# A seam in seven steps: its second transpose two slots ahead of its halves, and one product moved from GpSimd to VectorE

## Chip, cores, metric

One Trainium2 chip, one core. The metric is the device time of one execution in microseconds (us). The engines are called PE (TensorE), PEld (its weight loads), DVE (VectorE), ACT (ScalarE) and POOL (GpSimd).

## The reference

Induced attention on four sequences, then an RMS-normalised SwiGLU feed-forward layer on all 49,664 tokens, in fp32 (condensed):

```python
# x (4, 12416, 128), inducing (32, 128); w_gate, w_val (128, 1536); w_out (1536, 128)
def mab(q, kv):
    s = scale * (q @ kv.transpose(0, 2, 1))
    s = s - s.max(-1, keepdims=True)
    a = np.exp(s)
    a /= a.sum(-1, keepdims=True) + 1e-09
    return a @ kv
h = mab(I, x)            # 32 rows per sequence
y = mab(x, h)            # back to 12416 rows; then, on (49664, 128):
rms = np.sqrt(np.mean(y * y, axis=-1, keepdims=True) + 1e-06)
xn = y / rms * rms_g
g = xn @ w_gate
return ((g * (1.0 / (1.0 + np.exp(-g)))) * (xn @ w_val)) @ w_out
```

As `y` is a combination of 32 rows of `h`, the kernel multiplies `h` with the gate and value weights once per sequence. The feed-forward loop then needs only the attention weights `a` of each token, scaled so that the row of `y` that they make has an RMS of 1. Making those scaled weights is the seam.

## The kernel before

The seam of one group of 2048 tokens, as six steps. Each step is put into the instruction stream at a position of the group before: one pass of the loop below is a slot, and the 48 slots of a group are its positions 0 to 47. The last step makes the two halves, hi and lo, of the turned weights.

```python
def seam(b, s):
    ...
    engine = nc.gpsimd if b or s else nc.vector
    ...
    def turn_a():
        eT = st["eT"] = work.tile([P, 512], F32, name="eT", tag="work")
        nc.vector.transpose(out=eT[rows, 0:w], in_=sc[b][rows, cols2[s]])

    def square():
        ...
        nc.tensor.matmul(ps[rows, 0:w], gram[b][rows, rows], st["eT"][rows, 0:w], start=True, stop=True)

    def turn_z():
        ...
        nc.vector.transpose(out=z[rows, :, :].rearrange("p t m -> p (t m)"), in_=ps[rows, 0:w])
        engine.tensor_tensor(out=z[rows, :, :], in0=z[rows, :, :], in1=weights(b, s), op=ALU.mult)

    def scale():        # sum of z, then ms ** -0.5 on POOL
        ...
        nc.gpsimd.tensor_tensor(out=rs, in0=ms, in1=mhalf[rows, 0:n], op=ALU.pow)

    def apply():        # weights *= rs, in place in sc
        ...
        engine.tensor_tensor(out=a, in0=a, in1=rs.unsqueeze(2).to_broadcast(...), op=ALU.mult)

    def split():
        aT = work.tile([P, 512], F32, name="aT", tag="work")
        nc.vector.transpose(out=aT[rows, 0:w], in_=sc[b][rows, cols2[s]])
        ...
        nc.scalar.copy(out=hi[rows, 0:w], in_=aT[rows, 0:w])          # the cast of hi, on ACT
        ...
        engine.tensor_tensor(out=lo[rows, 0:w], in0=aT[rows, 0:w], in1=hi[rows, 0:w].bitcast(F32), op=ALU.subtract)

    return [turn_a, square, turn_z, scale, apply, split]
```

The loop body, and the operands of a split projection:

```python
def three(j, t):
    ...
    nc.scalar.activation(hi, v, AF.Copy, scale=1.0 - 2.0 ** -13)                    # ACT
    nc.gpsimd.tensor_tensor(out=lo, in0=v, in1=hi.bitcast(F32), op=ALU.subtract)    # POOL
    def rest():
        hs = third.tile([P, 512], F32, name="hs")
        nc.scalar.activation(hs[:, 0:T], hi.bitcast(F32), AF.Copy, scale=1.0 + 2.0 ** -12)
        nc.gpsimd.tensor_tensor(out=d, in0=hs[:, 0:T], in1=v, op=ALU.subtract)      # POOL, the third operand
        kara.append((ready[b, u, j], lambda: project3(j, hi, lo, d)))
    soon(1, rest)

for j in range(NJ):                                   # one slot
    nc.tensor.matmul(g[:, 0:T], sg[:, ts(j, P)], a[:, 0:T], start=True, stop=True)      # gate
    nc.scalar.activation(sl[:, 0:T], g[:, 0:T], AF.Silu)
    products(j)                                       # projections that are due
    nc.tensor.matmul(v[:, 0:T], sv[:, ts(j, P)], a[:, 0:T], start=True, stop=True)      # value
    nc.vector.tensor_tensor(out=t[:, 0:T], in0=sl[:, 0:T], in1=v[:, 0:T], op=ALU.mult)  # u
    steps(j)                                          # seams, prologue of the next sequence, ...
    ...
```

Where the steps stand, and the build-time reckoning of POOL's time that decides which projections are split (`SLOT` 1.25 us, `SPLIT` 2.75 us):

```python
j = ((14, 17, 18, 21, 21, 33) if k else (32, 33, 33, 34, 34, 37))[i]
...
seam_busy[at] = seam_busy.get(at, 0) + {2: 1.4, 3: 3.0, 4: 1.2, 5: 1.4}.get(i, 0)
...
free = max(free, now) + busy.get(k, 0) + seam_busy.get((b, u, j), 0)
begin = max(free, now + 2.2 * SLOT)
if (j not in KJ or b == 0 and u < 2 or (b, u) == flat[-1] or begin > now + 3.2 * SLOT or
        any(k - 2 <= e <= k + 6 for e in marks)):
    continue                                          # stays plain
free = begin + SPLIT
ready[b, u, j] = int((free + 0.3) / SLOT) + 1
```

## Time and profile before

| | before |
|---|---|
| time, median of 4 runs | 1710.03 us (1708.84 to 1710.2) |
| span of the profiled execution | 1708.1 us, granted clock 0.995 |
| busy share | PE 98%, ACT 72%, DVE 67%, POOL 67% |
| first gate matmul | 59.8 us after the start |
| ACT's cast of hi waiting for the turn | 40.2 us in 27 waits |

Most of these rows say little about where a microsecond can be had: PE looks full. One more place matters below, the first seam inside the loop. Lines of the timeline, before (start and duration in us; the bracket is the wait ahead of the instruction and what ended it):

```profile
131.21 2.90 POOL L499 TENSOR_TENSOR rs<-ms,mhalf 128x16 f32<-128x16 f32 x1
...
134.19 1.05 POOL L503 TENSOR_TENSOR sc<-sc,rs 128x512 f32<-128x512 f32 x1
135.20 1.26 POOL L603 TENSOR_TENSOR xn<-hs,u 128x512 fp32r<-128x512 f32 x1
...
136.52 0.50 PE L560 MATMUL acc<-xn,xn 128*128 128x512 f32 x1 [2.69 <-POOL xn L603]
```

PE stands still for 2.69 us for the third operand of a split projection, which stood behind the seam's power and apply in POOL's queue. Below I call this the standstill.

### The profile page before, as it was taken

Reading aid. Unit: us, or ns where it says so; the run is one execution under the profiler, and the core shown is the slowest. Engines: PE = TensorE matmul, PEld = TensorE weight load, DVE = VectorE, ACT = ScalarE, POOL = GpSimd, SP = SyncE. Lnnn points to the kernel's source line nnn. Section 1 sums busy time; section 2 is a strip of 40 time slices with the busy share of each in tenths; the row PEclk is TensorE's granted clock in tenths of the full one; section 3 lists DMA queues with packets and bytes.
Section 4 is the critical chain, followed back from the end, with each engine's and each line's share of the span. In section 5 each row is a group of like instructions: output and inputs, shape, how many; then the busy total and the mean of one; then the engine's idle time right before and its main releaser. Section 6 shows DMA issues by size and latency. Waiting matters only on the chain.

```text
span 1708.1 us, 23142 instructions
## 1 busy us (share of the span) xinstructions
PE 1668.0 (98%) x6781; PEld 1036.0 (61%) x6781; DVE 1145.0 (67%) x1914; ACT 1224.3 (72%) x2179; POOL 1146.2 (67%) x919
## 2 busy tenths in 40 slices
PE   8799999999999999999999999999999999999998
PEld 7445565655566666665556666566556666666666
DVE  4767775676667776667666777566756666666665
ACT  4446777676787777766678777767677887788786
POOL 1217775677587777677658777577657878887774
PEclk9899999999999999999999999999999999999999
DMA  6344533533354332433335314153211111111111
GB/s 261 74 68 75 70 80 60 121 75 69 56 78 68 49 65 51 105 75 88 65 57 90 57 34 87 28 131 79 54 31 33 35 36 33 33 36 36 33 37 24
DMA packets 389358, 112.64 MB, mean 66 GB/s; under 512 B 365136, under 2 KB 369776, under 8 KB 386672
## 3 DMA queue, kind: packets, MB, share of 16 engines
q1 hardware_dynamic: 388944, 111.02, 33.1%
q8 instruction: 54, 0.88, 0.2%
q14 instruction: 72, 0.59, 0.1%
q10 hardware_dynamic: 288, 0.15, 0.0%
HBM read 53.95 MB, written 27.00 MB: 47 GB/s over the span
## 4 chain that ended last, share of the span: by engine, by line
PE 87%; ACT 4%; DVE 3%; issue 2%; POOL 2%; DMA 1%; SPq 1%; ACTq 0%; DVEq 0%; POOLq 0%
PE acc L560 40%; PE gv L610 16%; PE gv L615 14%; PE u L578 5%; PE u L576 5%; PE mm L310 2%; DVE u L617 1%; PE mm L485 1%; ACT silu L612 1%; PE mm L368 1%; DVE aT L507 1%; PE gv L301 1%; ACT hi L510 1%; ACT hs L602 1%; POOL xn L603 1%
## 5 line engine op out<-in xcount | busy, mean ns | idle before, releaser
L617 DVE TENSOR_TENSOR u<-silu,gv 128x512 f32<-128x512 f32 (+2 forms) x1200 | 790.7, 666 | 512.1 <-PE gv L615 262.6
L612 ACT ACTIVATE silu<-gv 128x512 f32<-128x512 f32 (+2 forms) x1200 | 696.6, 584 | 370.1 <-PE gv L610 326.2
L560 PE MATMUL acc<-u,wo 128*128 128x512 f32 (+2 forms) x1634 | 811.5, 581 | 4.4 <-DVE u L617 3.1
L615 PE MATMUL gv<-a,sv 128*128 128x512 f32 (+2 forms) x1200 | 774.1, 645 | 3.7 <-DVE u L617 3.5
L598 POOL TENSOR_TENSOR xn<-u,xn 128x512 fp32r<-128x512 f32 (+2 forms) x383 | 482.2, 1259 | 356.0 <-ACT xn L597 295.1
L610 PE MATMUL gv<-a,sg 128*128 128x512 f32 (+2 forms) x1200 | 490.2, 409 | 12.8 <-ACT silu L612 8.5
L603 POOL TENSOR_TENSOR xn<-hs,u 128x512 fp32r<-128x512 f32 (+2 forms) x383 | 481.9, 1258 | 23.2 <-ACT hs L602 22.0
L610 PEld LDWEIGHTS gv<-a,sg 128*128 128x128 f32 x1200 | 227.2, 189 | 259.3 <-ACT silu L612 127.5
L560 PEld LDWEIGHTS acc<-u,wo 128*128 128x128 f32 x1634 | 305.1, 189 | 84.6 <-issue 18.2
L615 PEld LDWEIGHTS gv<-a,sv 128*128 128x128 f32 x1200 | 227.2, 189 | 204.1 <-issue 141.9
L597 ACT ACTIVATE xn<-u 128x512 fp32r<-128x512 f32 (+2 forms) x383 | 237.0, 619 | 15.6 <-DVE u L617 13.9
L602 ACT ACTIVATE hs<-xn 128x512 f32<-128x512 f32 (+2 forms) x383 | 235.7, 615 | 4.5 <-POOL xn L603 3.1
L560 PE MATMUL acc<-xn,xn 128*128 128x512 f32 (+2 forms) x383 | 149.7, 391 | 6.1 <-POOL xn L603 6.1
L578 PE MATMUL u<-xn,xn 128*128 128x512 f32 (+2 forms) x383 | 149.2, 390 | 0.0
L576 PE MATMUL u<-xn,xn 128*128 128x512 f32 (+2 forms) x383 | 147.8, 386 | 0.0
L499 POOL TENSOR_TENSOR rs<-ms,mhalf 128x16 f32<-128x16 f32 (+2 forms) x28 | 75.5, 2696 | 35.3 <-DVE ms L497 34.9
L560 PEld LDWEIGHTS acc<-xn,xn 128*128 128x128 f32 x383 | 71.8, 187 | 25.7 <-POOL xn L603 10.5
L578 PEld LDWEIGHTS u<-xn,xn 128*128 128x128 f32 x383 | 71.9, 188 | 15.6
L576 PEld LDWEIGHTS u<-xn,xn 128*128 128x128 f32 x383 | 72.1, 188 | 14.0
L569 DVE STREAM_TRANSPOSE o<-o 128x512 f32<-128x512 f32 (+2 forms) x97 | 67.7, 698 | 3.4
L568 DVE TENSOR_TENSOR o<-acc,o 128x512 f32<-128x512 f32 (+2 forms) x97 | 64.9, 669 | 0.0
L581 ACT ACTIVATE o<-u 128x512 f32<-128x512 f32 (+2 forms) x97 | 56.4, 581 | 0.2
(153 smaller groups left out, 735.0 us busy)
## 6 DMA issues: line engine op xcount, KB each, us to landing
out_dram<-o SPq DMA_DIRECT2D x320, 64.0 KB, 2.0
xT<-in_x_dram SPq DMA_DIRECT2D x60, 256.0 KB, 4.9
xn<-in_x_dram SPq DMA_DIRECT2D x60, 256.0 KB, 4.7
a<-hi SPq DMA_DIRECT2D x160, 64.0 KB, 2.0
a<-lo SPq DMA_DIRECT2D x158, 64.0 KB, 2.0
w<-w SPq DMA_DIRECT2D x22, 256.0 KB, 3.2
xn<-in_x_dram SPq DMA_DIRECT2D x5, 1024.0 KB, 10.9
out_dram<-o SPq DMA_DIRECT2D x64, 60.0 KB, 2.0
```

The lines of the kernel that those rows point to most:

```text
L499: nc.gpsimd.tensor_tensor(out=rs, in0=ms, in1=mhalf[rows, 0:n], op=ALU.pow)
L560: nc.tensor.matmul(acc[:, 0:T], lhsT, rhs, start=st["left"] == NJ, stop=st["left"] == 1)
L576: nc.tensor.matmul(ups[:, 0:T], w[:, i, :], hi, start=st["k"] == nk, stop=False)
L578: nc.tensor.matmul(ups[:, 0:T], w[:, NK + i, :], lo, start=False, stop=not st["k"])
L597: nc.scalar.activation(hi, v, AF.Copy, scale=1.0 - 2.0 ** -13)
L598: nc.gpsimd.tensor_tensor(out=lo, in0=v, in1=hi.bitcast(F32), op=ALU.subtract)
L602: nc.scalar.activation(hs[:, 0:T], hi.bitcast(F32), AF.Copy, scale=1.0 + 2.0 ** -12)
L603: nc.gpsimd.tensor_tensor(out=d, in0=hs[:, 0:T], in1=v, op=ALU.subtract)
L610: nc.tensor.matmul(g[:, 0:T], sg[:, ts(j, P)], a[:, 0:T], start=True, stop=True)
L612: nc.scalar.activation(sl[:, 0:T], g[:, 0:T], AF.Silu)
L615: nc.tensor.matmul(v[:, 0:T], sv[:, ts(j, P)], a[:, 0:T], start=True, stop=True)
L617: nc.vector.tensor_tensor(out=t[:, 0:T], in0=sl[:, 0:T], in1=v[:, 0:T], op=ALU.mult)
```

## The change

Intent: ACT, which works its queue in order, shall not meet the cast of hi before its input exists; so the second transpose becomes a step of its own, two slots ahead of the cast. And POOL shall lose the product z: DVE multiplies straight from PSUM with the already turned weights and then turns the product in place, which gives the same numbers. The reckoning of POOL's time loses the 1.4 us for z, and the halves' 1.4 us move to their new position.

```diff
@@ -488,8 +488,9 @@
             ps = st["ps"]
             lent.clear()
             z = st["z"] = work.tile([P, n, m], F32, name="z", tag="work")
-            nc.vector.transpose(out=z[rows, :, :].rearrange("p t m -> p (t m)"), in_=ps[rows, 0:w])
-            engine.tensor_tensor(out=z[rows, :, :], in0=z[rows, :, :], in1=weights(b, s), op=ALU.mult)
+            flat = z[rows, :, :].rearrange("p t m -> p (t m)")
+            nc.vector.tensor_tensor(out=flat, in0=ps[rows, 0:w], in1=st["eT"][rows, 0:w], op=ALU.mult)
+            nc.vector.transpose(out=flat, in_=flat)
 
         def scale():
             ms = numbers("ms")
@@ -502,9 +503,12 @@
             rs, a = st["rs"], weights(b, s)
             engine.tensor_tensor(out=a, in0=a, in1=rs.unsqueeze(2).to_broadcast((rs.shape[0], n, m)), op=ALU.mult)
 
+        def turn_b():
+            aT = st["aT"] = work.tile([P, 512], F32, name="aT", tag="work")
+            nc.vector.transpose(out=aT[rows, 0:w], in_=sc[b][rows, cols2[s]])
+
         def split():
-            aT = work.tile([P, 512], F32, name="aT", tag="work")
-            nc.vector.transpose(out=aT[rows, 0:w], in_=sc[b][rows, cols2[s]])
+            aT = st["aT"]
             hi, lo = split_of[b, s] = [halves.tile([P, 512], F32R, name=k) for k in ("hi", "lo")]
             if b or s:
                 nc.scalar.copy(out=hi[rows, 0:w], in_=aT[rows, 0:w])
@@ -512,7 +516,7 @@
                 nc.vector.tensor_copy(out=hi[rows, 0:w], in_=aT[rows, 0:w])
             engine.tensor_tensor(out=lo[rows, 0:w], in0=aT[rows, 0:w], in1=hi[rows, 0:w].bitcast(F32), op=ALU.subtract)
 
-        return [turn_a, square, turn_z, scale, apply, split]
+        return [turn_a, square, turn_z, scale, apply, turn_b, split]
 
     def gather(b, u):
 
@@ -680,7 +684,7 @@
     f["exp2"](0, 1)
     tiny = small.tile([P, 1], F32, name="tiny")
     nc.scalar.activation(tiny[:], ones[:], AF.Silu)
-    turn_a, square, turn_z, scale, apply, split = seam(0, 0)
+    turn_a, square, turn_z, scale, apply, turn_b, split = seam(0, 0)
     turn_a()
     square()
     join(0, 1)
@@ -693,6 +697,7 @@
     parts(1, 1)
     place(1, 1)
     apply()
+    turn_b()
     split()
     gather(0, 0)
     f["stack_of"](0, 1)
@@ -774,11 +779,11 @@
             following = order[k + 1:k + 3]
         for late_by, one in enumerate(following):
             for i, step in enumerate(seam(*one)):
-                j = ((14, 17, 18, 21, 21, 33) if k else (32, 33, 33, 34, 34, 37))[i]
+                j = ((14, 17, 18, 21, 21, 29, 31) if k else (32, 33, 33, 34, 34, 36, 38))[i]
                 n, j = divmod(j, NJ)
                 at = (b, firsts[s] + n + late_by, j)
                 seams.setdefault(at, []).append(step)
-                seam_busy[at] = seam_busy.get(at, 0) + {2: 1.4, 3: 3.0, 4: 1.2, 5: 1.4}.get(i, 0)
+                seam_busy[at] = seam_busy.get(at, 0) + {3: 3.0, 4: 1.2, 6: 1.4}.get(i, 0)
     flat = [(b, u) for b in range(B) for u in range(NU)]
     after = dict(zip(flat, flat[1:]))
     plans = [schedule(b) for b in range(B)]
```

## The prediction

> **What bounds the kernel now.** I read the page first (busy shares, then the chain of work that ended last), then the groups with shapes kept apart, the list of waits, and last the timeline around single seams.
>
> ```profile
> PE 1668.0 (98%) x6781; PEld 1036.0 (61%) x6781; DVE 1145.0 (67%) x1914; ACT 1224.3 (72%) x2179; POOL 1146.2 (67%) x919
> ...
> PE 87%; ACT 4%; DVE 3%; issue 2%; POOL 2%; DMA 1%; SPq 1%; ACTq 0%; DVEq 0%; POOLq 0%
> ```
>
> TensorE (PE) is 98% busy and 87% of the last chain. No other engine is above 72%. So a microsecond taken off POOL or VectorE (DVE) is worth nothing by itself; the change can gain only where it takes work off TensorE, or where TensorE stands still because of a seam.
>
> Some terms. The feed-forward loop runs in **slots**, 12 to a unit of 512 tokens, 1200 in all. A slot has a gate matmul, a value matmul, and on average one projection. A **plain** projection is two fp32 matmul records; a **split** one is three fp32r matmuls, for which ScalarE (ACT) and POOL first make three operands. A group is four units, **positions** 0 to 47. In each group the next group's attention weights pass through a seam: turn, square, z, scale, apply, turn again, halves. To see what a slot costs I take the time from one gate matmul's start to the next, because ends are modelled. A slot with a plain projection and the next kind, in the last batch:
>
> ```profile
> 1425.49 0.39 PE L610 MATMUL gv<-a,sg 128*128 128x512 f32 x1
> ...
> 1426.81 0.40 PE L610 MATMUL gv<-a,sg 128*128 128x512 f32 x1
> ...
> 1428.14 0.40 PE L610 MATMUL gv<-a,sg 128*128 128x512 f32 x1
> ...
> 1429.01 0.70 DVE L507 STREAM_TRANSPOSE aT<-sc 128x512 f32<-128x512 f32 x1
> ...
> 1429.31 0.40 PE L610 MATMUL gv<-a,sg 128*128 128x512 f32 x1
> ...
> 1429.75 0.62 ACT L510 CAST hi<-aT 128x512 fp32r<-128x512 f32 x1 [1.39 <-DVE aT L507]
> ...
> 1430.28 1.78 ACT L612 ACTIVATE silu<-gv 128x512 f32<-128x512 f32 x3
> ...
> 1430.92 0.19 PEld L610 LDWEIGHTS gv<-a,sg 128*128 128x128 f32 x1 [0.76 <-ACT silu L612]
> ```
>
> Two plain slots take 1.32 and 1.33 us, the split slot 1428.14 to 1429.31 takes 1.17 us. Over all undisturbed slots of the trace the medians are 1.325 and 1.160 us at 512 tokens, 1.240 and 1.079 at 480. The next slot, plain again, lasts from 1429.31 to 1430.92 = 1.61 us, 0.29 too long. The reason is in the same lines: ACT's queue holds the cast of hi, which waits 1.39 us for VectorE's turn of the weights, and three silu pile up behind it; TensorE then waits for a silu. This is the wait the change aims at. In the list of waits (total us, times, longest):
>
> ```profile
> ACT hi L510 <- DVE aT L507: 40.2, 27, 4.4
> ```
>
> It happens at all 27 seams inside the loop. ACT has slack, so only a part of the 40 us reaches TensorE.
>
> **What the Trainium skill says.** (1) "Perfetto Trace Analysis", Identifying the Most-Contended Engine: matmul busy share does not show how near TensorE is to its limit. The trace agrees: the 1.61 us slot counts as busy for most of its length, so I use start-to-start times. (2) "Trainium Architecture — The Big Picture", Inside one NeuronCore: each engine has an instruction stream of its own, and engines meet only through semaphores. The 1.39 us above shows the consequence here: silu that were ready stood behind the cast. (3) "GPSIMD Engine Reference", Elementwise: the same fp32 tensor_tensor costs GpSimd 1.96 times VectorE. Here it is 1281 ns against 682 ns for the u product with one input in PSUM, 1.88 times. (4) "SBUF — State Buffer", SBUF: two separate sides: a VectorE instruction with two SBUF inputs and a GpSimd one shut each other out. The new product reads PSUM and one SBUF tile, so I expect no such block; no run so far shows it.
>
> **The change, part by part.**
>
> *z.* Before, VectorE turns the square from PSUM and POOL multiplies it by the weights; after, VectorE multiplies from PSUM by the already turned weights and turns the product in place (the same numbers, as the turn permutes elements).
>
> ```profile
> L617 DVE TENSOR_TENSOR u<-silu,gv 128x512 f32<-128x512 f32 x960 | 648.4, 682 | 409.0 <-PE gv L615 208.7 <-ACT hs L602 71.1 <-ACT xn L597 66.0
> ...
> L492 POOL TENSOR_TENSOR z<-z,sc 128x512 f32<-128x512 f32 x19 | 24.3, 1281 | 12.2 <-ACT silu L612 10.8 <-DVE z L491 0.3
> ...
> L491 DVE STREAM_TRANSPOSE z<-mm 128x512 f32<-128x512 f32 x20 | 14.2, 710 | 0.3 <-PE mm L485 0.2
> ```
>
> POOL loses 24.3 us and the smaller shapes, about 32 us in all; VectorE gains one product of about 0.69 us per seam, 28 x 0.69 = 19 us, less the one 1.03 us product it did in the first seam. Both are beside TensorE.
>
> *More split projections.* The program decides at build time which projections are split, by a count of POOL's time. The seam's 1.4 us for z leaves that count, so it admits more. The instruction order of the two built programs gives it exactly: 383 split projections before, 400 after, 13 more at 512 tokens and 4 more at 480. Each turns a plain slot into a split one: 13 x 0.165 + 4 x 0.161 = 2.8 us off TensorE. POOL pays two operands for each, 13 x 2.58 + 4 x 2.44 = 43 us, so it ends some 11 us busier than before.
>
> *The turn two slots ahead.* The turn goes from position 33 to 29, the halves from 33 to 31. Is the turn's input ready by then? In the seam above POOL's apply ran from 1417.59 to 1418.64, while the gate of position 29 started at 1421.85, so there are 3 us to spare. The cast then finds its input ready, and the stall goes. I summed slot length minus the shortest slot of the same content. The stall is 0.24 to 0.31 us at position 35 in two groups of each of the first three batches and in five of the last, and 0.41 in the batches' sixth group, at position 47: 3 x (0.31 + 0.25 + 0.41) + 4 x 0.30 + 0.24 = 4.4 us. Group 2 of the first three batches has 0.75 + 0.37, mixed with the exp that begins there; I take about half, 3 x 0.6 = 1.8. At the other seams nothing reaches TensorE. An excess of 0.41 at position 18 everywhere is none: the square's tail is counted in the slot after it. Sum: 6.2 us.
>
> *POOL's order at position 18.* In group 4 of the first three batches z's product stands before the operand of a split projection:
>
> ```profile
> 797.38 1.05 POOL L417 TENSOR_TENSOR sc<-sc,mx 128x512 f32<-128x512 f32 x1
> 798.39 1.21 POOL L492 TENSOR_TENSOR z<-z,sc 128x480 f32<-128x480 f32 x1
> 799.56 1.28 POOL L603 TENSOR_TENSOR xn<-hs,u 128x512 fp32r<-128x512 f32 x1
> ...
> 800.89 0.51 PE L560 MATMUL acc<-xn,xn 128*128 128x512 f32 x1 [0.46 <-POOL xn L603]
> ```
>
> Without L492 that operand is ready 1.2 us earlier and the 0.46 us wait goes: 3 x 0.5 = 1.5 us.
>
> *Prologue and first seam.* Before the first gate matmul everything is one chain, and z's part falls from 0.72 + 1.03 to 0.69 + 0.71: 0.35 us. In the second seam (130 to 140 us) TensorE waits 2.7 us for a split operand that stands behind the seam's pow and apply on POOL; with z gone these start about 0.4 us earlier. Sum: 0.8 us.
>
> *Given back.* At position 18 VectorE now holds up the next u product by 1.40 us in place of 0.71, and a new split projection at position 19 waits for just that u. Followed through the seam above: that u would end at about 1412.0, and the value matmul that needs its PSUM buffer starts near 1412.3. It fits by 0.3 us; where it doesn't, a tenth or two is lost. I put 1.3 us for 23 seams.
>
> Sum: 2.8 + 6.2 + 1.5 + 0.8 - 1.3 = 10.0 us. 1710.1 - 10.0 = 1700.1, say **1700 us**.
>
> **Rivals.** *A: VectorE's longer block becomes the wait.* If the 0.3 us margin does not hold, each of 23 seams loses about 0.3 us, 7 us in all: 1706. For it: the last engine before u's delay is VectorE itself, and finished outputs (0.68 + 0.71 us) fall near it. Against: VectorE idles 0.6 us before most u products. *B: POOL is late.* After the new projection at position 19 comes the pow (2.90 us), then apply, then the operands for positions 24, 26 and 29; POOL ran without a gap from 1414.61 to 1423.6 already. If the pow starts 0.7 us later, every one of these has about 1 us left by my reading, since the schedule also gives two of them a slot more. If that is wrong, TensorE waits 0.5 us at 23 seams, 11 us, and the gain is gone: 1711. *C: more is gained.* The clock falls to half for 3.4 us after the second seam's standstill ("TensorE: Matmul & The Clock Gate" describes such windows, and this trace's record of the clock has one from 137.4 to 140.8 us). If a shorter standstill avoids it, 1.7 us more, and group 2 may give its whole 1.1: together about 3 us, 1697.
>
> **Range and chances.** C and a smaller give-back set the lower end, A nearly the upper: 1695 to 1707 us. 2% is 34 us; all seam stalls and new splits together are a third of that, and no rival costs more than 12. So within 2% is nearly certain: faster by over 2% 0.01, within 2% 0.98, slower 0.01.
>
> **What would show it.** Right, step by step: 400 records each of the three split matmuls; the 40.2 us wait of ACT's cast for the turn falls to a few; slots at position 35 of the last batch take their undisturbed length; no 0.46 us wait near 800 us; POOL about 1157 us busy, VectorE about 1163. Wrong: TensorE's waits for POOL's L603 line rise (B), value matmuls wait for u near position 21 (A), or the cast's wait moves to VectorE's turn waiting for apply at position 29. The size would be wrong first in the second step, where I took the recorded slot excess as all recoverable.

## The result, and the profile after

| | before | after |
|---|---|---|
| median (range of 4 runs) | 1710.03 us (1708.84 to 1710.2) | 1695.79 us (1694.02 to 1696.75) |
| ratio | | 0.9917, 95% interval 0.99 to 0.9934 |
| span of the profiled execution, clock | 1708.1 us, 0.995 | 1694.8 us, 0.995 |

A ratio is the mean time of one kernel's fast runs over the mean of the other's of the same rounds, so it is not quite the ratio of the medians that I quote. The change is a gain of 14.2 us, within 2%, and in the predicted range.

The lines of the page after the change (busy us, share, instructions; then the last chain by engine), and what is left in the list of waits:

```profile
PE 1661.3 (98%) x6798; PEld 1041.8 (61%) x6798; DVE 1167.6 (69%) x1941; ACT 1236.8 (73%) x2213; POOL 1158.5 (68%) x926
...
PE 92%; ACT 2%; DVE 2%; issue 2%; POOL 1%; DMA 1%; ACTq 0%; SPq 0%; DVEq 0%; POOLq 0%
```

```profile
ACT hi L514 <- DVE aT L508: 1.5, 1, 1.5
```

ACT and POOL fell from 4% and 2% of the last chain to 2% and 1%, PE rose from 87% to 92%: less of the end is set by others. The cast's waits fell from 40.2 us in 27 to a single one of 1.5 us. The same seam of the last batch as in the prediction, after:

```profile
1412.85 0.70 DVE L508 STREAM_TRANSPOSE aT<-sc 128x512 f32<-128x512 f32 x1
...
1413.13 0.39 PE L614 MATMUL gv<-a,sg 128*128 128x512 f32 x1
...
1414.46 0.40 PE L614 MATMUL gv<-a,sg 128*128 128x512 f32 x1
...
1414.64 0.61 ACT L514 CAST hi<-aT 128x512 fp32r<-128x512 f32 x1
...
1415.62 0.40 PE L614 MATMUL gv<-a,sg 128*128 128x512 f32 x1
...
1416.95 0.39 PE L614 MATMUL gv<-a,sg 128*128 128x512 f32 x1
```

The turn ends a whole slot before the cast, which starts without a wait. The slots are 1.33, 1.16 and 1.33 us: undisturbed ones of both kinds, no 1.61 any more.

**Where the time came from.** I cut both traces at the gate matmuls and compared the length of each group (after minus before, us):

| batch | group 0 | 1 | 2 | 3 | 4 | 5 | 6 |
|---|---|---|---|---|---|---|---|
| 0 | -0.61 | -0.53 | -0.85 | -0.17 | -1.08 | -0.59 | -0.04 |
| 1 | -0.15 | -0.55 | -0.86 | -0.17 | -1.09 | -0.58 | -0.03 |
| 2 | -0.13 | -0.53 | -0.88 | -0.17 | -1.10 | -0.59 | +0.08 |
| 3 | -0.50 | -0.53 | -0.52 | -0.53 | -0.47 | -0.18 | 0.00 |

The sum is -13.4 us; the spans differ by 13.3. The table is easy to read: a group that only gained one split projection is 0.13 to 0.18 us shorter (group 3 of the first three batches, group 0 of the second and third, group 5 of the last); groups 2 and 4 of the first three batches gained no split and only lost stalls; the others show both.

### The profile page after: what moved, and what is told of

Same layout as the page of the kernel before. It is cut to its first block, busy times and chain, and to the rows that moved or that the text cites. A ratio compares the mean times of both kernels' runs of the same rounds, so it can differ in the third digit from the quotient of the medians.

```text
span 1694.8 us, 23289 instructions
## 1 busy us (share of the span) xinstructions
PE 1661.3 (98%) x6798; PEld 1041.8 (61%) x6798; DVE 1167.6 (69%) x1941; ACT 1236.8 (73%) x2213; POOL 1158.5 (68%) x926
## 4 chain that ended last, share of the span: by engine, by line
PE 92%; ACT 2%; DVE 2%; issue 2%; POOL 1%; DMA 1%; ACTq 0%; SPq 0%; DVEq 0%; POOLq 0%
PE acc L564 42%; PE gv L614 16%; PE gv L619 15%; PE u L582 5%; PE u L580 5%; PE mm L310 3%; PE mm L485 1%; PE mm L368 1%; DVE u L621 1%; PE gv L301 1%; ACT silu L616 1%; DMA xn<-in_x_dram 1%; ACT L616 1%; PE gv L310 0%; PE acc L181 0%
## 5 line engine op out<-in xcount | busy, mean ns | idle before, releaser
L564 PE MATMUL acc<-u,wo 128*128 128x512 f32 (+2 forms) x1600 | 793.7, 580 | 3.6 <-DVE u L621 2.2
L619 PE MATMUL gv<-a,sv 128*128 128x512 f32 (+2 forms) x1200 | 766.0, 638 | 3.8 <-DVE u L621 3.6
L602 POOL TENSOR_TENSOR xn<-u,xn 128x512 fp32r<-128x512 f32 (+2 forms) x400 | 504.9, 1262 | 365.7 <-ACT xn L601 331.2
L607 POOL TENSOR_TENSOR xn<-hs,u 128x512 fp32r<-128x512 f32 (+2 forms) x400 | 503.9, 1260 | 37.7 <-ACT hs L606 35.2
L564 PEld LDWEIGHTS acc<-u,wo 128*128 128x128 f32 x1600 | 298.6, 189 | 83.0 <-issue 19.0
L601 ACT ACTIVATE xn<-u 128x512 fp32r<-128x512 f32 (+2 forms) x400 | 247.8, 620 | 26.8 <-DVE u L621 24.9
L606 ACT ACTIVATE hs<-xn 128x512 f32<-128x512 f32 (+2 forms) x400 | 246.8, 617 | 5.5 <-POOL xn L607 4.0
L564 PE MATMUL acc<-xn,xn 128*128 128x512 f32 (+2 forms) x400 | 156.1, 390 | 4.6 <-POOL xn L607 4.6
L582 PE MATMUL u<-xn,xn 128*128 128x512 f32 (+2 forms) x400 | 155.8, 389 | 0.0
L580 PE MATMUL u<-xn,xn 128*128 128x512 f32 (+2 forms) x400 | 154.4, 386 | 0.0
L580 PEld LDWEIGHTS u<-xn,xn 128*128 128x128 f32 x400 | 75.2, 188 | 16.3 <-issue 0.7
L582 PEld LDWEIGHTS u<-xn,xn 128*128 128x128 f32 x400 | 75.1, 188 | 16.2
```

What stands on the lines that cost most here:

```text
L564: nc.tensor.matmul(acc[:, 0:T], lhsT, rhs, start=st["left"] == NJ, stop=st["left"] == 1)
L580: nc.tensor.matmul(ups[:, 0:T], w[:, i, :], hi, start=st["k"] == nk, stop=False)
L582: nc.tensor.matmul(ups[:, 0:T], w[:, NK + i, :], lo, start=False, stop=not st["k"])
```

## The experiments

My theory after the result: the gain is the sum of separate repairs, namely the cast's wait (largest), a POOL operand that no longer stands behind z, and more split projections. Rivals: *A* (the prediction's A), DVE's longer block of 1.4 us at position 18 costs time that was made up elsewhere; *D* (not the prediction's B), POOL's relief is what counts, and moving the turn is incidental. In several kernels the reckoning of POOL's time is kept as it was, so that the same 383 projections are split; the others have 400 unless I say otherwise. All kernels gave correct results.

The medians scatter, in part with the granted clock: the runs of the kernel before at a mean clock of 0.996 took 1708.2 to 1709.3 us, those at 0.993 or 0.994 took 1709.9 to 1710.4. In the profiled runs of these kernels the first gate matmul came 58.5 to 59.9 us after the start; in the six traces with a stretch of half clock near 11 us the exp before the first seam began at 45.6 to 46.1 us, in the other seven at 44.6 to 45.2. So I also give the sum over the loop, and this table of the group changes against the kernel before (us; groups 1 to 5 are means over the first three batches, "last" the mean of groups 0 to 4 of the last batch):

| kernel | 1 | 2 | 3 | 4 | 5 | last | whole loop |
|---|---|---|---|---|---|---|---|
| the change | -0.54 | -0.86 | -0.17 | -1.09 | -0.59 | -0.51 | -13.4 |
| e1_turn_only | -0.40 | -0.81 | 0.00 | +0.33 | -0.45 | -0.39 | -6.4 |
| e2_z_only | 0.00 | 0.00 | 0.00 | -0.77 | -0.05 | 0.00 | -4.8 |
| e3_both_383 | -0.40 | -0.80 | 0.00 | -0.40 | -0.46 | -0.38 | -8.8 |
| e4_splits_only | -0.08 | +0.17 | -0.17 | +0.07 | +0.55 | -0.14 | +2.1 |
| e5_together_31 | +0.63 | +0.47 | +0.82 | +0.21 | +0.75 | +0.03 | +6.8 |
| e12_turn_31_halves_33 | -0.40 | -0.81 | 0.00 | -1.11 | -0.45 | -0.38 | -11.0 |

The whole loop also holds the first group of the first batch. In e2 and e5 it is 2.4 us shorter than before, most of it by a half clock that did not come (last section); without it their loops are -2.4 and +9.2 us.

### The turn alone: e1_turn_only

z stays with POOL, 383 split projections as before (against the changed kernel):

```diff
-            nc.vector.tensor_tensor(out=flat, in0=ps[rows, 0:w], in1=st["eT"][rows, 0:w], op=ALU.mult)
-            nc.vector.transpose(out=flat, in_=flat)
+            nc.vector.transpose(out=z[rows, :, :].rearrange("p t m -> p (t m)"), in_=ps[rows, 0:w])
+            engine.tensor_tensor(out=z[rows, :, :], in0=z[rows, :, :], in1=weights(b, s), op=ALU.mult)
@@ the reckoning of before
-                seam_busy[at] = seam_busy.get(at, 0) + {3: 3.0, 4: 1.2, 6: 1.4}.get(i, 0)
+            for j, cost in zip((18, 21, 21, 33) if k else (33, 34, 34, 37), (1.4, 3.0, 1.2, 1.4)):
+                n, j = divmod(j, NJ)
+                at = (b, firsts[s] + n + late_by, j)
+                seam_busy[at] = seam_busy.get(at, 0) + cost
```

> The turn two slots ahead of the halves alone; z stays on POOL, the 383 split projections are the old ones. My theory (the cast's wait was most of the gain): slot excess at positions 35 and 47, and at 35 and 36 of group 2, falls by 7.6 us as between the two traces, so 1702.4 us; ACT's wait for the turn falls from 40 us to under 8; the 0.75 us excess at position 22 of group 4 stays. Rival (the stall went because POOL had less to do): under 2 us gained, 1708 or more, and the excess at position 35 stays.

Measured: 1703.8 us, ratio 0.9964 (0.9949 to 0.9979) to 1709.88 of before. ACT's cast waits 1.5 us in all, and the excess at positions 35 and 47 is gone in every group that had it. So D falls: with z still on POOL, groups 1, 2, 5 and the last batch give what they give in the full change, less 0.05 to 0.14 us, at most about one split's worth. But group 4 became longer, by a new wait at position 36 that I had not foreseen. Timeline of e1, group 4 of the first batch:

```profile
813.56 1.22 POOL L516 TENSOR_TENSOR lo<-aT,hi 128x480 fp32r<-128x480 f32 x1
814.73 1.32 POOL L601 TENSOR_TENSOR xn<-u,xn 128x512 fp32r<-128x512 f32 x1
815.99 1.07 POOL L417 TENSOR_TENSOR sc<-sc,mx 128x512 f32<-128x512 f32 x1
817.00 1.30 POOL L606 TENSOR_TENSOR xn<-hs,u 128x512 fp32r<-128x512 f32 x1
...
818.35 0.50 PE L563 MATMUL acc<-xn,xn 128*128 128x512 f32 x1 [0.41 <-POOL xn L606]
```

With the halves at 31, POOL makes lo ahead of the operands of a split projection, and with the next sequence's subtraction (L417) these four fill POOL without a gap; the third operand comes last and PE waits. The slot is 0.69 us too long. The reckoning in this kernel still believes that the halves come at 33.

### z alone: e2_z_only

The changed kernel with turn and halves together at 33, and 383 splits:

```diff
-                j = ((14, 17, 18, 21, 21, 29, 31) if k else (32, 33, 33, 34, 34, 36, 38))[i]
+                j = ((14, 17, 18, 21, 21, 33, 33) if k else (32, 33, 33, 34, 34, 37, 37))[i]
@@ and the reckoning of before, as in e1_turn_only
```

> z by VectorE alone; turn and halves together at position 33 as before, old 383 split projections. My theory: only the 0.75 us at position 22 of group 4 goes, three times, and 0.3 us of the prologue: 1707.4 us; ACT's wait for the turn stays near 40 us and the 0.30 us at position 35 of the last batch stays. Rival A (VectorE's longer block at position 18 costs TensorE): 0.1 to 0.3 us lost at each of 23 seams, 1710 to 1714 us, with excess at positions 20 to 23.

Measured: 1706.4 us, ratio 0.9981 (0.9966 to 0.9996). The cast waits as it did, 39.3 us in 27 waits. Only group 4 gained, 0.77 us in each of three batches; every group whose seam DVE now blocks for 1.4 us stayed within 0.06 us. So with the old splits A falls as well: the longer block costs nothing. They lack the split at position 19, which A was about; e3 and e6 bear on that. (In this run the first group is 2.4 us shorter. Most of that is luck with the clock: see the last section.)

The repair in group 4, in the full change, for comparison with the four lines around 797 us in the prediction:

```profile
792.86 1.28 POOL L607 TENSOR_TENSOR xn<-hs,u 128x512 fp32r<-128x512 f32 x1
...
794.73 0.40 PE L564 MATMUL acc<-xn,xn 128*128 128x512 f32 x1
```

The subtraction ran from 791.85 to 792.90, so nothing stands between it and the operand, and PE's matmul has no wait.

### Both moves, old choice of splits: e3_both_383

The changed kernel with the reckoning of before (the diff's second half in e1_turn_only).

> Both parts, but with the old 383 split projections. My theory: the parts add, 7.6 + 2.25 + 0.3 us below before, about 1699.7 us, and 2.8 to 3.9 us above the changed kernel, which is the worth of the 17 further splits. Rival (the further splits pay for themselves only in part, POOL being late for them): within 1.5 us of the changed kernel.

Measured: 1700.07 us, ratio 0.9944 (0.9929 to 0.9959). The group changes of e1 and e2 add up (group 4: +0.33 - 0.77 = -0.44, measured -0.40), so the two moves do not interact, and position 36 of group 4 still costs 0.69 us. What the new choice of splits adds is then 1700.07 - 1695.79 = 4.3 us, or 4.6 in the loop of the two traces: 2.5 in the seventeen groups that gain a split (0.11 to 0.18 each), and 3 x 0.69 = 2.1 because it drops the split at position 31 of group 4 and takes the one at 33, which avoids the queue shown above.

### The new choice of splits alone: e4_splits_only

The kernel before with the 400 splits of the changed one:

```diff
-                seam_busy[at] = seam_busy.get(at, 0) + {2: 1.4, 3: 3.0, 4: 1.2, 5: 1.4}.get(i, 0)
+            for j, cost in zip((21, 21, 31) if k else (34, 34, 38), (3.0, 1.2, 1.4)):
+                n, j = divmod(j, NJ)
+                at = (b, firsts[s] + n + late_by, j)
+                seam_busy[at] = seam_busy.get(at, 0) + cost
```

> The kernel before, with the changed kernel's choice of 400 split projections and nothing else changed: z on POOL, turn and halves together at 33. My theory (the splits need the POOL time that z gave up): each is worth 0.165 us, but POOL's queue between positions 18 and 32 is over-full by about 1 us a group and TensorE waits for the third operand; 1709 to 1713 us, TensorE's waits for that operand's line up from 17 us by several us. Rival (the count alone did it): 2.8 us faster than before, 1707.2 us, with no new wait.

Measured: 1711.33 us, ratio 1.0011 (0.9994 to 1.0027): no gain. Each new split still saved 0.12 to 0.17 us in group 3 and in the last batch, but groups 5 and 6 of the first three batches lost 0.55 us each, and group 2 lost 0.17. PE's weight loads wait longer for the third operand, 16.6 us in 28 waits against 10.5 us in 14 before. List of waits of e4 (total us, times, longest):

```profile
PEld acc L560 <- POOL xn L603: 16.6, 28, 3.1
```

And e4's timeline at position 22 of group 5:

```profile
869.44 0.72 POOL L492 TENSOR_TENSOR z<-z,sc 32x256 f32<-32x256 f32 x1
...
870.13 1.20 POOL L603 TENSOR_TENSOR xn<-hs,u 128x480 fp32r<-128x480 f32 x1
...
871.39 0.49 PE L560 MATMUL acc<-xn,xn 128*128 128x480 f32 x1 [0.51 <-POOL xn L603]
```

The operand of a split projection stands behind z again. So the splits are not free-standing: they were worth their 2.5 us only together with the two moves. No run separates which of the two makes the room; at this place it was z that stood in the way.

### Position or distance: e5_together_31 and e12_turn_31_halves_33

Is the gain from the halves' earlier position, or from the distance between turn and cast? Both with 383 splits; turn and halves at 31, and turn at 31 with the halves where they were:

```diff
# e5_together_31
+                j = ((14, 17, 18, 21, 21, 31, 31) if k else (32, 33, 33, 34, 34, 36, 38))[i]
# e12_turn_31_halves_33
+                j = ((14, 17, 18, 21, 21, 31, 33) if k else (32, 33, 33, 34, 34, 36, 38))[i]
```

> z by VectorE, the old 383 splits, turn and halves both at position 31 inside the loop: two slots earlier than before, but not apart. My theory (what counts is the distance between VectorE's turn and ACT's cast): ACT still waits about 1.4 us for the turn at each seam, 35 to 40 us in all, and the 0.30 us excess appears two positions earlier, at 33; near the run with z alone, 1704.5 to 1709 us. Rival (being earlier in the group is enough): near the run with both parts and 383 splits, 1700 us, with no excess at 33 to 35 in the last batch.

> z by VectorE, old 383 splits, the halves left at position 33 as before and only the turn drawn ahead of them, to 31. If the distance is what counts: ACT's wait for the turn is gone (under 6 us), no 0.30 us excess at 33 or 35, and the 0.69 us at position 36 of group 4, which came when the halves moved to 31 beside the old splits, is not there: 1698 us, about 2 us under the run with both parts and 383 splits. If the earlier halves counted: 1705 us or more.

Measured: e5 1717.38 us, ratio 1.0048 (1.0033 to 1.0063), slower than before; e12 1698.74 us, ratio 0.9936 (0.9921 to 0.9951). I expected e5 to lose its gain, not to lose more than before. The timeline of one of its seams (group 1 of the second batch):

```profile
609.25 0.67 DVE L508 STREAM_TRANSPOSE aT<-sc 128x512 f32<-128x512 f32 x1
...
609.95 0.62 ACT L514 CAST hi<-aT 128x512 fp32r<-128x512 f32 x1 [1.84 <-DVE aT L508]
610.47 0.59 ACT L616 ACTIVATE silu<-gv 128x512 f32<-128x512 f32 x1
...
611.12 0.19 PEld L614 LDWEIGHTS gv<-a,sg 128*128 128x128 f32 x1 [1.23 <-ACT silu L616]
```

The cast waits about as long in total as in the kernel before (38.0 us in 27 waits, against 40.2 in 27), yet the loop is 6.8 us longer, 9.2 without the lucky first group: a wait's total does not tell what reaches PE. e12 settles the question: the halves at their old position, the turn two slots ahead of them, and all the stalls at positions 33 to 36 are gone, in group 4 too. So the distance did it; the earlier position of the halves added nothing and, with the old splits, cost 0.69 us three times. (With the new splits, halves at 33 were not tried.) Why a joint step at 31 hurts the first three batches more than one at 33 I did not settle.

### How much room DVE has: e6_block_one and e7_block_two

The changed kernel with one, or two, more DVE turns after z, into a buffer that nobody reads any more (0.71 us each):

```diff
             nc.vector.transpose(out=flat, in_=flat)
+            nc.vector.transpose(out=st["eT"][rows, 0:w], in_=flat)      # e6: once, e7: twice
```

> The changed kernel with one further VectorE turn (0.71 us, into a tile nobody reads again) behind z's turn, so that VectorE is held 2.1 us at position 18. It measures the margin that my give-back of 1.3 us rested on. In the changed kernel u of position 19 ends about 0.7 us before its PSUM buffer is wanted, so: nothing lost to 0.2 us a seam, 1695.5 to 1700 us. Rival A with the margin of 0.3 us that I wrote: 0.4 us lost at each of 23 seams, 1705 us.

> The same with two further turns, VectorE held 2.8 us. The margin is used up: TensorE waits at positions 20 to 22 for a PSUM buffer, 0.5 to 0.9 us at each of 23 to 27 seams, 1707 to 1718 us. If nothing at all is lost, the u product at position 18 was never near TensorE's path.

Measured: e6 1700.94 us, ratio 0.9953 (0.9938 to 0.9968), one microsecond above what I had allowed; e7 1714.98 us, ratio 1.0034 (1.0019 to 1.0049). In the quiet seams of the last batch e6 costs 0.2 us each and e7 0.96 us each. 0.71 - 0.21 = 0.50 and 1.42 - 0.96 = 0.46: the room there was just under half a microsecond, where I had read 0.3 from one seam. In the first three batches it was not the same everywhere: groups 3 and 4 had more (0 to 0.2 us lost even in e7), group 5 less (0.28 to 0.69 us lost in e6, 1.2 to 1.9 in e7, part of it at position 33). Timeline of e7 in a seam of the last batch:

```profile
1416.96 1.25 DVE L623 TENSOR_TENSOR u<-silu,gv 128x512 f32<-128x512 f32 x2
...
1417.66 0.19 PEld L616 LDWEIGHTS gv<-a,sg 128*128 128x128 f32 x1 [1.08 <-DVE u L623]
```

There is rival A, made real: the gate's weight load waits 1.08 us for the late u. The mechanism that I priced at 1.3 us exists; the change stops short of nearly all of it.

### The standstill of the first group: e8_drop_first, e10_first_group

The changed kernel has the standstill as before, only half a microsecond earlier: its matmul waited 2.70 us, against the 2.69 shown above.

```profile
136.00 0.50 PE L564 MATMUL acc<-xn,xn 128*128 128x512 f32 x1 [2.70 <-POOL xn L607]
```

e8 leaves out the one split projection whose operand PE waits for; e10 then also moves the first group's turn and halves later (39 and 41) and the gather of the next unit's weights with them, and so has 401 splits:

```diff
# e8_drop_first and e10_first_group
-            if (j not in KJ or b == 0 and u < 2 or (b, u) == flat[-1] or begin > now + 3.2 * SLOT or
+            if (j not in KJ or b == 0 and u < 3 or (b, u) == flat[-1] or begin > now + 3.2 * SLOT or
# e10_first_group
-                j = ((14, 17, 18, 21, 21, 29, 31) if k else (32, 33, 33, 34, 34, 36, 38))[i]
+                j = ((14, 17, 18, 21, 21, 29, 31) if k else (32, 33, 33, 34, 34, 39, 41))[i]
-                if j == 2 and (b, u) in after:
+                if j == (6 if (b, u) == (0, 3) else 2) and (b, u) in after:
```

> The changed kernel without the split projection of position 33 in the very first group, whose third operand stands behind pow and apply on POOL (the choice then puts one at position 36 instead; 400 in all). Its wait of 2.7 us and the half clock behind it go: slot excess at 38 to 40 falls from 4.6 us to under 1, 3 to 4 us faster than the changed kernel, 1692 to 1693 us. If the wait only moves to another slot of that group: no change.

> The changed kernel; in the very first group no split projection at position 33, the turn at 39, the halves at 41 and their transfers begun at 42, so that neither VectorE nor ACT stands in line for POOL's pow and apply. Dropping the split alone left a 2.7 us standstill one slot later, by VectorE's turn at 36 waiting for apply. Theory: excess at positions 36 to 41 of that group falls from 4.6 us to under 1.5, 3 us or more faster than the changed kernel: 1692 us, and the half clock near 137 us is gone. Rival: the transfers come late for the next unit and the standstill moves to its first gate matmul: no gain.

Measured: e8 1694.77 us, ratio 0.9911 (0.9895 to 0.9928), which the change's own interval overlaps; e10 1692.77 us, ratio 0.9899 (0.9883 to 0.9916). In e8 the standstill moved:

```profile
134.42 0.71 DVE L508 STREAM_TRANSPOSE aT<-sc 128x512 f32<-128x512 f32 x1 [2.30 <-POOL sc L504]
...
135.76 1.12 PE L564 MATMUL acc<-u,wo 128*128 128x512 f32 x2 [2.43 <-DVE u L621]
```

Now it is DVE's queue that holds an instruction without its input: the turn waits 2.30 us for POOL's apply, u stands behind it, and PE waits for u. This is the same fault that the change repairs on ACT, on another engine: an early step in an in-order queue. With the turn three slots later (e10) the standstill is gone: the first group is 4.8 us shorter than in the changed kernel, of which 0.9 comes back in group 1, to which some of its work moved. The half clock behind the standstill is gone too, 1.7 us of the 4.8 by the estimate of the last section. The three edits of e10 were not tried one by one.

### The best version: e11_and_submax

e10 with the subtraction that was left ahead of an operand in group 4 given to DVE:

```diff
-            (nc.gpsimd if s else nc.vector).tensor_tensor(
+            (nc.gpsimd if s and s != 4 else nc.vector).tensor_tensor(
                 out=v, in0=v, in1=mx.unsqueeze(2).to_broadcast((mx.shape[0], n, m)), op=ALU.subtract)
```

> The run before this, and the subtraction of the maximum in group 4 moved from POOL to VectorE: it stood ahead of the third operand of a split projection and cost 0.88 us at position 43 in each of the first three batches. Theory: 3 x 0.6 to 0.9 us, 1.8 to 2.6 us faster than the run without it: about 1689.7 us. Rival: VectorE's 0.7 us delay a u product there and nothing or less than 1 us is left.

Measured: 1689.4 us, ratio 0.9882 (0.9867 to 0.9896); group 4 is 0.88 to 0.90 us shorter in each of the first three batches than in e10. The wait that goes, in the changed kernel's timeline, and the same place in e11:

```profile
823.73 1.05 POOL L417 TENSOR_TENSOR sc<-sc,mx 128x512 f32<-128x512 f32 x1 [0.78 <-PE gv L614]
...
824.74 1.28 POOL L607 TENSOR_TENSOR xn<-hs,u 128x512 fp32r<-128x512 f32 x1
...
826.07 0.50 PE L564 MATMUL acc<-xn,xn 128*128 128x512 f32 x1 [0.62 <-POOL xn L607]
```

```profile
816.71 1.31 POOL L607 TENSOR_TENSOR xn<-hs,u 128x512 fp32r<-128x512 f32 x1
...
817.50 1.06 DVE L417 TENSOR_TENSOR sc<-sc,mx 128x512 f32<-128x512 f32 x1
...
819.10 0.40 PE L564 MATMUL acc<-xn,xn 128*128 128x512 f32 x1
```

This version is faster than both kernels: 20 us below the kernel before, 6 us below the change.

## Why the prediction was right

The direction and the mechanism were right; the sum was 4.2 us too small (10.0 against 14.2 measured, 13.3 in the profiled spans). That it lay inside the range is in part luck: the range's lower end leaned on the avoided half clock of C, which did not come. A larger gain from the cast's wait and a smaller give-back stood in for it. By its own terms, the loop's 13.4 us taken apart with the table of groups:

| term | predicted | measured |
|---|---|---|
| more split projections | 2.8 | 2.5 (from e3 to the change, in the 17 groups that gain a split) |
| the cast's wait | 6.2 | 8.0 (e1, without the new wait in group 4) |
| POOL's order at position 18 | 1.5 | 2.3 (e2) |
| prologue and second seam | 0.8 | 0.6 in the loop; 0.3 in the prologue, hidden |
| given back | -1.3 | at most 0.3, already taken off the 2.5 |
| sum | 10.0 | 13.4 |

- **More split projections.** 400 records, as forecast; e3 and the change differ in this choice alone. What the prediction did not say: they are worth that only together with the two moves. Alone (e4) they gave nothing.
- **The cast's wait.** The mechanism is shown by e1 and e12. The size was the largest error, 1.8 us. In e1 groups 1, 4 (with the 0.69 us added back) and 5 gave 0.40, 0.36 and 0.45 us, 0.04 to 0.11 more than their excess in the trace; group 2 gave 0.81 where I took 0.6, about half of what was mixed with an exp. That half was too cautious: 3 x 0.21 = 0.6 us of the 1.8 missing. The last batch gave 1.95 us where I had 1.44.
- **POOL's order at position 18.** The wait is gone, and e2 shows it alone: 0.77 us a group. I took the wait that the profile puts before the matmul, 0.46; the slot's excess was 0.75. By my own measure (slot length, not recorded wait) I should have taken the latter.
- **Prologue and second seam.** From the exp to the first gate matmul the prologue fell from 14.15 to 13.83 us, 0.32 as against 0.35 predicted (13.8 us in all eight traces with z on DVE and no extra turn, 14.15 or 14.16 in the three with z as before); in this run the exp itself came 0.4 us later, so nothing of it shows in the span. The standstill comes 0.5 us sooner but is as long as before, and the first group is 0.6 us shorter.
- **Given back.** Too large by 1.0 to 1.3 us. The mechanism is real (e7), but the room in the last batch was nearly 0.5 us, and in e2, with the old splits, no group grew by more than 0.03 us. With the split at position 19 something is lost after all: 2.5 us for the new splits against 2.8 computed, and in group 5 of the second batch slots 22 and 25 are 0.1 us longer than in e3. That all of the 0.3 us is this loss is not shown. A margin read from one seam was right in sign and too small in size, and I should not have charged 23 seams for it.
- **Rivals.** A, at 0.3 us a seam, is refuted: e2 shows no loss with the old splits, and with the new ones at most 0.3 us is lost in all. B does not occur (in the change PE's weight loads wait 8.5 us in all for the third operand, 10.5 before). C, the avoided half clock, did not come with this change, as the standstill stayed. In e2 and e5 it did, with a standstill as long as before: the length alone does not decide (last section).
- **Not foreseen.** The halves at 31 next to the old splits cost 0.69 us at position 36 of group 4 (e1, e3). The new choice of splits happens to avoid it, so the full change never shows it.

## What to carry to other kernels

An instruction that waits in an in-order queue holds up everything behind it; put the producer ahead of such a consumer (two slots here, the only distance tried), and look at every engine's queue for the same fault, since removing it on one can uncover it on the next (e8). Read the size of a stall from the length of the loop's slot against an undisturbed slot of the same content, not from the recorded wait or from the list's total: 40.2 us of waits here were worth 8.0, and almost the same total in e5 went with a loop 6.8 us longer. When work moves, run the scheduler's reckoning again with the new places: without it the two moves were worth 4.3 us less (e3), and the new reckoning was worth nothing without them (e4).

## What the Trainium skill lacked or had wrong

- "TensorE: Matmul & The Clock Gate", What's actually happening: it gives half rate after at least one idle window of about 3.4 us, and calls the window free-running. Here a standstill of 2.4 to 2.7 us, shorter than that, was followed by about 3.4 us at half the granted clock in the kernel before, the change and seven experiments, but not in e2 and e5 with the same standstill. The free-running phase agrees with that; the threshold does not hold as a bound. In each trace all changes in the clock record lie on a grid of 3.413 us. I cut all 13 traces on their grids: of 6391 steps at full clock, the 49 in which PE idled over 1.91 us were all followed by half clock, the 6330 with under 1.6 us never, and the 12 between went either way. The standstill put 1.97 to 2.70 us of idle time into one step in those nine traces; in e2 and e5 the grid cut it in two, with at most 1.72 and 1.56 us in a step. So in these traces some half of one step idle was enough. Busy time by stretch for the kernel before, then for e2 (the last columns are PEclk, the DMA share and GB/s):

```profile
137.50:140.50 3.00, 3.00 (x5) 1.38 (x5) 2.55 (x4) 1.11 (x3) 0.49 (x1) 0.50 0.30 69
```

```profile
137.50:140.50 3.00, 3.00 (x12) 1.78 (x11) 2.93 (x5) 1.20 (x2) 0.00 (x0) 1.00 0.29 67
```

  In the same 3 us PE issued 5 matmuls in one and 12 in the other. It is worth some 1.7 us (half of 3.4, an estimate; slots 39 and 40 of that group are together 1.67 us longer before than in e2) and explains most of the 2.4 us by which e2's first group was shorter.
- "SBUF — State Buffer", SBUF: two separate sides: the shared port is right as far as it goes. The product of z reads PSUM and one SBUF tile, took 685 ns beside a busy POOL, and POOL's operands took 1.29 us before and after: no block. The subtraction with two SBUF inputs in e11 took 1.06 us beside a POOL operand, 0.70 us in the prologue of the kernel before. It ended 0.55 us after POOL's operand did in each of its three instances. The trace shows the block only as such a longer duration, not as a wait; the page could say so.
- No page gives the cost of GpSimd's power: here 2.90 us for 128x16, more than twice a 128x512 product (1.28 us). It is the longest of the three POOL instructions that make the standstill.
- "GPSIMD Engine Reference", Elementwise: 1.96 times VectorE's time; at 128x512 the runs show 1.88 (1281 against 682 ns). Right, with a slightly smaller factor for a smaller tile and an input in PSUM.
- No page says what three fp32r matmuls cost against one fp32 product: here a slot of 1.160 us against 1.325 at 512 tokens.
